# Four state heads side by side in the matmul array: a transformer block with linear attention on one core

## The chip, the cores and the metric

The kernel runs on one core of a Trainium2 chip. The core has a matmul engine (TensorE, PE in the profile; its weight loads are shown as PEld), VectorE (DVE), ScalarE (ACT), GpSimd (POOL) and a queue engine, SyncE (SP), that issues transfers. The metric is the device time of one execution in microseconds; less is better.

## The reference

A block on x of 2048 tokens by 640 features in bf16: layer norm, linear attention with 32 heads of 20 features, a residual, layer norm, a SiLU network of 1728, a residual.

```python
qkv = (x @ wqkv).reshape(B, S, 3, H, Dh)             # x: layer norm of the input
pq, pk = q @ w_phi, k @ w_phi                         # per head, 20 x 20
phi_q = concat([softmax(pq), softmax(-pq)])
phi_k = concat([softmax(pk), softmax(-pk)])
kv = einsum("bhsf,bhsd->bhfd", phi_k, v); z = phi_k.sum(s)
o = (phi_q @ kv) / (phi_q @ z + 1e-6)
h = x0 + o @ wo
out = h + silu(layernorm(h) @ w1) @ w2
```

## The kernel before

Tokens lie in 16 tiles of 128. The kernel is a list of small operations (`op_..`), and the string `ORDER` names them one after the other; each word appends its instructions to the queues of the engines that they use, so this one string fixes the order on PE, DVE, ACT, POOL and SP alike. An engine works its own queue strictly in that order. A word's last part can choose an engine or a queue: `lk.2.3.a` loads wk slice 2 from ACT's queue, `lk.2.3.s` from SP's. A transfer signals completion on one of eight counters, which are given out in turn; a transfer that gets a counter a second time first waits on its own engine's queue for the counter's last transfer to land.

Loads: `lx` (x tiles), `lk`, `lv` (slices of the k and v weights, 128 of the 640 input features each), `lp` (w_phi, 40-byte rows), `lq` (q weights, transposed by the transfer), `lo`, `l1`, `l2`, `lh`.

*First stage.* The per-head matrices w_phi are folded into the k and q weights: PE transposes five wk slices (`wt`, L293), ACT or DVE copies them out (`wc`), PE multiplies with w_phi spread to a block matrix (`fk`, `gk`, L308), and a copy makes Wfk and Wfq (`fc`, `gc`). Every key projection needs all five slices of Wfk. `wm` (L241) are matmuls on zeros that only keep PE busy at the start. For each token tile: statistics (`st` on DVE, `rs` on POOL), normalization (`xn`), transpose on PE (`xt`) or by a transfer (`xd`); key projection `kp` and value projection `vp` (both L336); exponentials of both signs on ACT (`ke`, L358); sums and reciprocals on DVE (`kr`, L366, L369); normalization on POOL (`kn`, L376). The state product `cc` (L394) adds kv over all tokens: for each sign and five column groups, two halves of the array (64 columns each) take 64 of the 640 features and multiply them with the values of four heads that these features touch, 84 columns. It also computes products between different heads; `km` (L404) masks them away and writes KVBD, with a column for the softmax sums of the queries.

*Second stage.* `qp` (L414) projects queries (128 features by 512 tokens), `qe` (L424) takes exponentials of both signs. The query-state product `dp` (L448) runs in two row halves of 64 features, 88 columns each, ten pairs a token tile, into two pairs of PSUM banks, one for each sign. `dw` on DVE combines the signs (L461, L462, L464 reads the negative pair, L468 the positive one), `dr` (L477) inverts, `do` (L483) scales, `td` transposes by a transfer, `op` (L510) multiplies with wo, `oa` (L519) adds the residual, `sq`, `sr`, `hn`, `hd` make the second norm and its transpose.

*Network.* `up` (L581, and L591 for the last 64 features), `ua` (L603), `yp` and `yh` (L627, L642), `yo` and `yz` (add and store).

PSUM has eight banks; a pool of four pairs hands them out.

Of the kernel before, what the change touches and what calls it, by code (L numbers as in the profile page):

```python
# [25 lines left out]
lx.0.1.s lk.4.5.a lp.s lk.3.4.a lx.1.2.s lk.2.3.a mk ta wt.4 wc.4.a wt.3 wm.256 st.0 rs.0.1 wt.2 ph  # L26
wm.256 wc.3.a lx.2.4.s wc.2.a fk.4 wm.256 fc.4.a st.1 lv.3.5.a xn.0.v wm.256 wm.256 wm.256 wm.256
st.2 lk.1.2.s wt.1 wc.1.v fk.2 lk.0.1.s rs.1.2 lx.4.8.s wt.0 wc.0.v xt.0 lv.0.3.s xc.0.v rs.2.3
xn.2.v xn.1.v mc st.3 rs.3.4 st.5 st.4 st.6 fc.2.a rs.4.6 fk.1 st.7 fc.1.a wm.256 fk.0 wm.256
lx.8.12.s st.8 st.9 fk.3 st.11 st.10 wm.512 fc.0.a rs.6.8 rs.8.10 xt.2 fc.3.a xt.1 xc.2.a xn.9.v  # L30
kp.0 ke.0 xc.1.a xn.3.a kp.2 lq.0 lq.4 vp.2 lx.12.16.s st.13 vc.2.a vp.0 vp.1 xt.3 xn.5.a xn.8.v
vc.0.a xn.4.a vc.1.a xc.3.a xn.7.a st.12 ke.2 kp.1 rs.10.12 kr.0 vp.3 vc.3.a mo rs.12.14 ke.1 kn.0
xd.5 kp.5 ke.5 xn.11.v kr.5 kn.5 st.14 st.15 rs.14.16 kp.3 ke.3 gk.0 kr.3 kn.3 xd.4 kp.4 ke.4 xd.7
xd.8 kp.7 ke.7 xn.10.a gc.0.a kr.2 kn.2 xn.13.a kr.4 kr.7 kp.8 kn.4 kn.7 vp.8 vc.8.a vp.5 xd.9
l2.8.13.s kr.1 vp.4 ke.8 kr.8 kn.8 lo.s kp.9 xd.11 kp.11 vc.5.a vc.4.a xn.12.a xn.6.a xn.14.a
xn.15.a vp.9 xd.13 cc.0 cc.3 vc.9.a ke.11 ke.9 cc.5 cc.2 lq.2 xd.10 vp.13 vc.13.v xd.6 vp.10 vc.10.a
kp.13 ke.13 kp.10 ke.10 lq.3 gk.3 vp.7 kp.6 cc.4 cc.8 vc.7.a cc.7 kr.11 ke.6 gc.3.v xd.14 lq.1 kr.13
kn.1 cc.1 kr.9 kn.11 xd.12 kp.14 ke.14 xd.15 kp.15 kn.9 ke.15 kr.6 kn.6 kr.10 kn.10 gk.1 gc.1.a
kp.12 vp.15 ke.12 kr.12 gk.2 vp.11 vc.15.a gk.4 gc.2.a gc.4.v kn.12 kr.15 vc.11.v vp.12 vc.12.a
qp.0.1 qe.0.1 vp.6 vc.6.a kn.15 kn.13 qp.0.0 kr.14 qp.0.2 vp.14 qe.0.2 cc.13 qe.0.0 cc.6 cc.9 cc.10  # L40
cc.15 cc.11 cc.12 vc.14.a kn.14 cc.14 close km.0 km.1 qp.2.2 qe.2.2 l1.2.s dp.0 dw.0.v dr.0 qp.3.2
qe.3.2 qp.1.2 dp.3 dw.3.v qe.1.2 do.0.1.p do.0.0.p td.0 dr.3 qp.1.0 qe.1.0 l1.1.s dp.1 dw.1.v dr.1
do.1.0.p do.1.1.p qp.1.1 qe.1.1 dp.2 dw.2.v qp.2.1 qe.2.1 dr.2 td.1 dp.4 do.2.0.p op.0 dw.4.v oa.0
op.1 oa.1 sq.1 do.2.1.p sq.0 td.2 dp.7 dw.7.v qp.2.0 qe.2.0 dp.5 dr.4 do.3.1.p do.3.0.p td.3
l2.4.8.s l1.0.s dw.5.v sr.0 do.4.1.p hn.0 hd.0 qp.3.1 dr.7 do.4.0.v dr.5 sr.1 hn.1 hd.1 dp.6 qe.3.1
qp.3.0 qe.3.0 dw.6.v lh.s op.3 do.5.0.p oa.3 dr.6 op.2 oa.2 do.5.1.p td.5 sq.3 sq.2 up.0.3 ua.0.3
do.7.1.p do.7.0.v td.4 l2.0.4.s dp.9 do.6.1.p up.0.2 ua.0.2 sr.2 dw.9.v dp.11 dw.11.v up.0.0 ua.0.0
sr.3 hn.3 hd.3 td.7 dp.8 hn.2 up.0.1 ua.0.1 dw.8.v dr.11 dr.9 dr.8 do.6.0.p do.8.1.p do.8.0.v op.5
oa.5 dp.10 yp.0.1 td.8 sq.5 sr.5 do.9.0.v dw.10.v op.4 oa.4 sq.4 do.11.1.v op.7 oa.7 hn.5 yp.1.0
sr.4 td.6 hd.2 do.11.0.v sq.7 hd.5 hn.4 hd.4 yp.0.0 dp.12 yh.0.0 dr.10 yp.1.1 dw.12.v yo.0 do.10.1.v  # L50
op.8 op.6 dr.12 do.10.0.p yo.1 oa.6 sq.6 sr.6 sr.7 up.1.2 do.9.1.v td.9 ua.1.2 td.10 hn.6 do.12.0.p
oa.8 sq.8 up.1.1 ua.1.1 sr.8 hn.8 hn.7 op.9 hd.6 hd.8 oa.9 sq.9 op.10 oa.10 sq.10 up.1.0 ua.1.0
up.1.5 ua.1.5 hd.7 up.1.3 ua.1.3 sr.9 hn.9 up.1.6 ua.1.6 dp.13 dw.13.v hd.9 up.2.3 ua.2.3 up.1.4
dp.15 dw.15.v dr.15 do.15.1.p ua.1.4 yp.4.0 dr.13 td.11 up.2.1 op.11 yp.4.1 ua.2.1 oa.11 dp.14
yh.1.0 dw.14.v do.12.1.p sr.10 do.15.0.p hn.10 yp.2.0 up.2.4 ua.2.4 td.15 td.12 op.15 oa.15 up.2.2
ua.2.2 sq.11 yo.4 yp.5.0 yp.5.1 sq.15 sr.15 hn.15 hd.15 do.13.0.v yp.2.1 yo.2 sr.11 yp.3.0 up.2.6
ua.2.6 yh.1.1 up.2.0 ua.2.0 op.12 hn.11 yo.5 do.13.1.p td.13 dr.14 up.2.5 do.14.1.v do.14.0.p ua.2.5
yp.8.0 yp.3.1 yo.3 td.14 yp.7.1 yp.7.0 oa.12 sq.12 yp.8.1 sr.12 op.13 oa.13 op.14 hn.12 yp.6.0
yp.9.1 yp.9.0 oa.14 hd.12 sq.13 sr.13 sq.14 sr.14 hn.14 hd.14 yh.2.0 yh.2.1 hn.13 hd.13 yp.6.1 yo.8
up.4.3 up.4.2 ua.4.2 up.4.1 ua.4.1 hd.10 hd.11 up.3.6 ua.4.3 up.4.0 yo.9 up.3.1 up.3.5 ua.4.0 ua.3.1  # L60
up.3.3 ua.3.3 up.3.2 up.3.0 ua.3.2 up.3.4 yp.15.0 yo.7 yo.6 yp.14.1 ua.3.6 yh.3.0 yh.4.0 ua.3.0
yp.14.0 yo.14 ua.3.5 ua.3.4 yp.12.0 yp.11.0 yp.10.1 yp.11.1 yp.10.0 yo.10 yp.12.1 yo.12 yp.15.1
yh.3.1 yo.11 yo.15 yq.13.0 yz.13.0.a yq.13.1 yz.13.1.a
# [3 lines left out]
def kernel(  # L67
# [29 lines left out]
    HQ = [(64 * q) // DH for q in range(2 * C)]  # L97
# [8 lines left out]
    mm = ctx.enter_context(tc.tile_pool(name="mm", bufs=4, space=PSUM))  # L106

    def mm2():
        return mm.tile([P, 2, 512], F32, name="mm2")

    def mmT():
        return mm.tile([P, C, P], BF16, name="mm2")
# [26 lines left out]
    maskS = persist.tile([P, C, 4, 1], BF16, name="maskS")  # L139
    KVBD = persist.tile([P, 2, C, 4, 22], BF16, name="KVBD")  # L140
# [19 lines left out]
    def wk2():  # L160
        return late["work"]
# [32 lines left out]
    def op_mc():  # L194
        nc.gpsimd.memset(maskS[:], 1.0)
        for lo in (0, 64):
            m = maskS[lo : lo + 64, :, :, 0]
            nc.gpsimd.affine_select(
                out=m, in_=m, compare_op=ALU.is_ge, fill=0.0,
                base=0, pattern=[[64 - 3 * DH, C], [-DH, 4]], channel_multiplier=1,  # L200
            )
            nc.gpsimd.affine_select(
                out=m, in_=m, compare_op=ALU.is_gt, fill=0.0,
                base=DH, pattern=[[3 * DH - 64, C], [DH, 4]], channel_multiplier=-1,
            )
        for s in range(2):
            nc.gpsimd.tensor_copy(KVBD[:, s, :, :, 21], maskS[:, :, :, 0])

# [17 lines left out]
    def op_lq(c):  # L226
        nc.sync.dma_start_transpose(wTq[:, :, c * P : (c + 1) * P], A_wqkv[c * P : (c + 1) * P, 0:D])
# [11 lines left out]
    def op_wm(n=512, ps=None):  # L239
        ps = mm2() if ps is None else ps  # L240
        nc.tensor.matmul(ps[:, 0, 0:n], ident[:], warm[:, 0:n], start=True, stop=True)  # L241
        return ps
# [82 lines left out]
    def op_gc(ce, eng="a"):  # L325
        copy(
            eng,
            Wfq[:, ce, :].rearrange("p (r a k) -> p a r k", r=C, a=2),
            tl["gk", ce][:, :, 0:320].rearrange("p a (r k) -> p a r k", r=C),
        )  # L330
# [13 lines left out]

    def op_vc(t, eng="a"):
        copy(
            eng,
            Vps[t % NV][:].rearrange("p (a h) c -> p a h c", a=2)[:, :, :, 0:DH],
            tl["vp", t][:, :, 0:320].rearrange("p a (h f) -> p a h f", f=DH),
        )  # L350
# [21 lines left out]
    def op_kn(t):  # L372
        Ek3 = tl["ek", t][:].rearrange("p s (h f) -> p (s h) f", f=DH)
        Sk = tl["sk", t]
        n = H if t == T - 1 else 2 * H
# [3 lines left out]
        if n == H:  # L379
            nc.vector.tensor_tensor(  # L380
                Ek3[:, n:], Ek3[:, n:], Sk[:, n:].unsqueeze(2).to_broadcast([P, n, DH]), op=ALU.mult,
            )

    def op_cc(t):
        Ek, Vp = tl["ek", t], Vps[t % NV]
        if "kv" not in tl:
            kv = mm2()
            tl["kv"] = [kv[:, s, 0:420].rearrange("p (r j c) -> p r j c", r=C, j=4) for s in range(2)]
        kv = tl["kv"]
        for s in range(2):  # L390
            for r in range(C):
                for a in range(2):
                    q, lo = C * a + r, 64 * a
                    nc.tensor.matmul(  # L394
                        kv[s][lo : lo + 64, r, :, :].rearrange("p j c -> p (j c)"),
                        Ek[:, s, 64 * q : 64 * q + 64],
                        Vp[:, HQ[q] : HQ[q] + 4, :].rearrange("p h c -> p (h c)"),
                        start=(t == 0 and r == 0),
                        stop=(t == T - 1),
                        skip_group_check=True,  # L400
                    )

    def op_km(s):
        nc.vector.tensor_tensor(  # L404
            KVBD[:, s, :, :, 0:21], tl["kv"][s], maskS[:].to_broadcast([P, C, 4, 21]), op=ALU.mult,
        )
# [3 lines left out]
    def op_qp(g, i):  # L410
        ps = mm2()
# [29 lines left out]
    def op_dp(t):  # L441
        g, i = t // GT, t % GT
        ps = [mm2(), mm2()]
        for s in range(2):
            for r in range(C):
                for a in range(2):
                    lo = 64 * a
                    nc.tensor.matmul(  # L448
                        ps[s][:, a, HQ[r] * 22 : (HQ[r] + 4) * 22],
                        EqT[g][lo : lo + 64, s, r, i * P : (i + 1) * P],  # L450
                        KVBD[lo : lo + 64, s, r, :, :].rearrange("p j c -> p (j c)"),
# [245 lines left out]
```

## Time and profile before

| | us |
|---|---|
| median of three runs (241.56 to 242.15) | 242.07 |
| span of the profiled execution, first to last instruction | 239.3 |
| first matmul starts | 1.52 |
| first key projection starts | 11.04 |
| last state product group starts | 66.22 |
| first query-state product starts | 70.58 |
| state products, busy, 320 matmuls | 6.7 |
| query-state products, busy, 320 matmuls | 9.1 |

In the page, a line of section 5 gives a group's busy time and mean ns of one instruction. A matmul's mean ns is its way through the array, and neighbours overlap; what a group costs is read from the timeline, as the distance from its start to the start of the next group. In a timeline line the first number is the start, the second the length, both in us; ACTq and SPq are the issuing of transfers. A wait line reads: total us, times, longest.

### The profile page before, as it was taken

The page shows a single profiled execution, that of the slowest core. Times are in us where ns is not written, and L with a number is a line of the kernel's source. Part 1 is how long each engine was busy: PE and PEld are TensorE (multiplying, and loading weights), DVE is VectorE, ACT ScalarE, POOL GpSimd, SP SyncE. Part 2 cuts the span into 40 slices and gives each one's busy share as a digit, 9 for nine tenths or more (in the row PEclk, how much of TensorE's full clock was granted, in tenths as well). Part 3 has the DMA queues.
Part 4 walks back from the last instruction along what each step waited for, and adds up shares of the span by engine and source line. Part 5 has one row for each costly group of instructions (what it writes and reads, how often), then busy time and mean ns, then how long its engine had stood idle before and what let it go on. Part 6 is the DMA issues. An engine that isn't in the chain of part 4 may idle for free.

```text
span 239.3 us, 5227 instructions
## 1 busy us (share of the span) xinstructions
PE 232.3 (97%) x2149; PEld 150.4 (63%) x2164; DVE 131.9 (55%) x253; ACT 108.6 (45%) x158; POOL 93.5 (39%) x183
## 2 busy tenths in 40 slices
PE   6989999999999999999999999999999999999995
PEld 2867777776574555877655455565577686456762
DVE  3999799887629999899653153424023410001033
ACT  4779997675566756733035531141312023270000
POOL 5868899978902456715145005022122200000000
PEclk9999999999999999999999999999999999999999
DMA  7995896700001659735244300202221390000012
GB/s 202 327 242 96 226 203 100 190 9 0 3 3 24 157 119 234 182 61 85 56 106 82 63 3 2 53 30 55 55 58 20 78 153 0 0 3 0 27 58 82
DMA packets 42808, 20.60 MB, mean 86 GB/s; under 512 B 34336, under 2 KB 42272, under 8 KB 42784
## 3 DMA queue, kind: packets, MB, share of 16 engines
q1 hardware_dynamic: 41792, 19.29, 35.9%
q10 hardware_dynamic: 992, 0.98, 1.2%
q8 instruction: 17, 0.28, 0.5%
q14 instruction: 7, 0.06, 0.1%
HBM read 9.61 MB, written 2.62 MB: 51 GB/s over the span
## 4 chain that ended last, share of the span: by engine, by line
PE 85%; DVE 7%; DMA 5%; issue 1%; ACTq 0%; ACT 0%; DVEq 0%
PE mm L581 24%; PE mm L627 24%; PE mm L336 17%; PE mm L510 8%; PE mm L414 5%; DMA wv<-in_A_wqkv_dram 3%; PE mm L394 3%; DVE u L464 2%; DVE u L468 2%; PE mm L448 2%; DMA wk<-in_A_wqkv_dram 2%; PE mm L591 1%; PE mm L642 1%; DVE w L461 1%; PE mm L308 1%
## 5 line engine op out<-in xcount | busy, mean ns | idle before, releaser
L581 PE MATMUL mm<-HnT,w 128*128 128x512 bf16 (+1 forms) x317 | 58.5, 336 | 0.4
L627 PE MATMUL mm<-w,shT 128*128 128x320 bf16 (+2 forms) x415 | 58.5, 299 | 0.2 <-issue 0.2
L603 ACT ACTIVATE shT<-mm 128x1024 bf16<-128x1024 f32 (+2 forms) x29 | 27.6, 963 | 51.8 <-PE mm L581 44.8
L627 PEld LDWEIGHTS <-shT 128*128 128x128 bf16 x416 | 39.7, 98 | 17.8 <-issue 1.3
L581 PEld LDWEIGHTS <-w 128*128 128x128 bf16 x325 | 31.3, 98 | 23.3 <-issue 0.5
L650 DVE TENSOR_TENSOR ob<-mm,X 128x640 bf16<-128x640 f32 x15 | 12.0, 817 | 50.2 <-PE mm L627 44.1
L336 PEld LDWEIGHTS <-XnT 128*128 128x128 bf16 x320 | 30.8, 98 | 12.9 <-issue 0.9
L376 POOL TENSOR_TENSOR Ek<-Ek,Sk 128x1280 bf16<-128x1280 bf16 (+1 forms) x16 | 36.8, 2325 | 3.7 <-DVE Sk L369 3.7
L483 POOL TENSOR_TENSOR o<-u,rd 128x320 bf16<-128x320 f32 x22 | 16.3, 758 | 38.8 <-DVE rd L477 30.6
L527 ACT ACTIVATE sq<-X 128x640 bf16<-128x640 bf16 x16 | 11.8, 736 | 30.0 <-DVE X L519 27.1
L424 ACT ACTIVATE EqT<-mm 128x1024 bf16<-128x1024 f32 (+1 forms) x24 | 19.7, 880 | 11.5 <-PE mm L414 11.4
L366 DVE TENSOR_REDUCE Sk<-Ek 128x64 f32<-128x1280 bf16 x16 | 23.2, 1450 | 2.8 <-ACT Ek L358 2.8
L336 PE MATMUL mm<-wv,XnT 128*128 128x320 bf16 x160 | 23.7, 299 | 0.7 <-DMA wv<-in_A_wqkv_dram 0.7
L510 PE MATMUL mm<-wo,ot 128*128 128x320 bf16 x160 | 23.5, 299 | 0.1
L414 PE MATMUL mm<-XnT,Wfq 128*128 128x512 bf16 x94 | 22.9, 379 | 0.4
L336 PE MATMUL mm<-Wfk,XnT 128*128 128x320 bf16 x160 | 23.2, 299 | 0.0
L358 ACT ACTIVATE Ek<-mm 128x640 bf16<-128x640 f32 x32 | 20.5, 730 | 4.0 <-PE mm L336 2.6
L510 PEld LDWEIGHTS <-ot 128*128 128x128 bf16 x160 | 15.5, 98 | 7.1 <-DMA ot<-o 0.3
L519 DVE SCALAR_TENSOR_TENSOR X<-mm,X 128x640 bf16<-128x640 f32 x16 | 13.0, 822 | 11.6 <-PE mm L510 11.4
L532 POOL TENSOR_SCALAR hm<-hst 128x1 f32<-128x1 f32 x16 | 3.9, 244 | 31.3 <-DVE X L519 31.3
L414 PEld LDWEIGHTS <-Wfq 128*128 128x128 bf16 x100 | 9.2, 97 | 10.2
L247 DVE BATCH_NORM_STATS2 stats<-X 128x6 f32<-128x320 bf16 x32 | 13.6, 466 | 2.7 <-DMA X<-in_A_x_dram 2.7
(74 smaller groups left out, 210.1 us busy)
## 6 DMA issues: line engine op xcount, KB each, us to landing
out_dram<-ob SPq DMA_DIRECT2D x15, 160.0 KB, 1.8
w<-in_B_w_dram SPq DMA_DIRECT2D x3, 720.0 KB, 4.6
X<-in_A_x_dram SPq DMA_DIRECT2D x3, 640.0 KB, 7.1
w<-in_B_w_dram SPq DMA_DIRECT2D x2, 640.0 KB, 5.1
w<-in_B_w_dram SPq DMA_DIRECT2D x1, 800.0 KB, 4.7
wo<-in_A_wo_dram SPq DMA_DIRECT2D x1, 800.0 KB, 7.6
wk<-in_A_wqkv_dram ACTq DMA_DIRECT2D x3, 160.0 KB, 3.5
wv<-in_A_wqkv_dram SPq DMA_DIRECT2D x1, 480.0 KB, 7.4
```

The source lines that it names most:

```text
L247: nc.vector.bn_stats(stats[:, k, :], X[:, t, k * 320 : (k + 1) * 320])
L336: nc.tensor.matmul(ps[:, half, 0:320], tok(XnT[t // GT], t)[:, c, :], W[:, c, half * 320 : (half + 1) * 320], start=(c == 0), stop=(c == C ...
L358: nc.scalar.activation(Ek[:, s, :].rearrange("p (a n) -> p a n", a=2), tl["kp", t][:, :, 0:320], AF.Exp, scale=1.0 - 2.0 * s,)
L366: nc.vector.tensor_reduce(Sk[:], tl["ek", t][:].rearrange("p s (h f) -> p (s h) f", f=DH), axis=AX.X, op=ALU.add,)
L376: nc.gpsimd.tensor_tensor(Ek3[:, 0:n], Ek3[:, 0:n], Sk[:, 0:n].unsqueeze(2).to_broadcast([P, n, DH]), op=ALU.mult,)
L414: nc.tensor.matmul(ps[:, k, :], Wfq[:, c, r * P : (r + 1) * P], XnT[g][:, c, :], start=(c == 0), stop=(c == C - 1),)
L424: nc.scalar.activation(E[:, s, rs[0] : rs[-1] + 1, :], tl["qp", g, i][:, 0 : len(rs), :], AF.Exp, scale=1.0 - 2.0 * s,)
L483: (nc.vector if eng == "v" else nc.gpsimd).tensor_tensor(tl["o", t][:, a * 320 : (a + 1) * 320].rearrange("p (h f) -> p h f", f=DH), tl["u ...
L510: nc.tensor.matmul(ps[:, half, 0:320], tl["ot", t][:, c, :], wo[:, c, half * 320 : (half + 1) * 320], start=(c == 0), stop=(c == C - 1),)
L581: nc.tensor.matmul(ps[:, i * W : (i + 1) * W], w1[:, c, fc * P : (fc + 1) * P], HnT[g][:, c, 0:W], start=(c == 0), stop=(c == C - 1), skip ...
L603: nc.scalar.activation(sh[:, a:b], tl["up", g, k][:, 0 : b - a], AF.Silu)
L627: nc.tensor.matmul(ps, shT[g][:, fc * W + i * P : fc * W + (i + 1) * P], w2[:, fc, a:b], start=first and fc == 0, stop=last and fc == FC - ...
```

## The change

- `cc`: one head is one tile of the array, 32 columns wide. The values of a head with a column of ones (21 columns) are loaded as weights and both signs of the head's exponentials pass (2 x 20 columns). Four heads, 8 apart, run in the four column tiles; eight rounds a token tile. All heads and signs gather in one bank (number 7). No product between different heads is computed here.
- `kc`, new: ACT copies that bank to SBUF as bf16, DVE transposes it in blocks of 32 x 32. `km` then spreads it with a mask over three heads, from SBUF instead of PSUM. The mask is made by other POOL operations (`mc`) and a DVE block transpose (`mt`).
- `dp`: four row tiles of 32 features instead of two of 64, two or three heads each (44 or 66 columns), into four banks at once; both signs lie in each of the four banks. 40 matmuls a token tile instead of 20.
- PSUM: no pool. The word's part after `@` names the bank; dp takes four, mostly 0 to 3.
- `gc` copies in two instructions instead of one, since the order of the query features changes (heads 8 apart share a group of 128).
- `kn` can be shared 48 to 16 or 32 to 32 of its 64 groups between POOL and DVE; four tiles use the first, one the second (before: one the second).
- `ORDER` is new for all engines. PE has 1026 more instructions; apart from cc and dp, its matmuls are the same in number and shape but for warm-up (17 instead of 16).
- In the head, the loads are issued otherwise. SP: wk slice 0, X tiles 2 and 3, wk slices 4, 1, 3, X tile 0, X tiles 12 to 15, wv 3 and 4, wv 0 to 2, X tiles 4 to 7. ACT: X tile 1, w_phi, then the table load with the first Exp (`ta`), then wk slice 2, later X tiles 8 to 11. In the built program slice 2 waits for the counter of slice 4, and SP's transfers from X tiles 12 to 15 on for the counters of X tile 1, slice 0, w_phi and X tiles 2 and 3 in turn. PE's first transposes are of slice 0, then slice 2, 4, 1, 3. The ones columns of the values (`mo`) are set first on POOL, before the masks.

The diff, cut to its core:

```diff
-lx.0.1.s lk.4.5.a lp.s lk.3.4.a lx.1.2.s lk.2.3.a mk ta wt.4 wc.4.a wt.3 wm.256 st.0 rs.0.1 wt.2 ph
-wm.256 wc.3.a lx.2.4.s wc.2.a fk.4 wm.256 fc.4.a st.1 lv.3.5.a xn.0.v wm.256 wm.256 wm.256 wm.256
...
+lx.1.2.a mo st.1 mk lk.0.1.s lp.a lx.2.4.s ta lk.2.3.a lk.4.5.s ph rs.1.2 wm.512@7 wm.512@7 wm.512@7
+wm.512@7 wm.512@7 wm.512@7 wt.0@0 wc.0.a wm.256@2 wm.256@2 wm.256@2 wm.256@2 wm.256@2 wm.256@2 wm.256@2
+wm.256@2 wm.256@2 wm.256@2 wt.2@1 wc.2.a st.2 rs.2.3 wm.256@3 wt.4@2 wc.4.a fk.0@4 fc.0.a lk.1.2.s wt.1@3
+st.3 rs.3.4 xn.1.v mc wc.1.v lk.3.4.s fk.2@6 lx.0.1.s fc.2.a wt.3@0 xt.1@1 fk.4@2 fk.1@4 fc.1.a fc.4.a
+wc.3.v fk.3@6 xn.2.v xt.2@0 xc.2.a xc.1.v xn.3.v xt.3@1 xc.3.a fc.3.v kp.1@4 kp.2@6 st.0 rs.0.1 lx.12.16.s
...
+kn.8.q cc.8 kn.6.b cc.6 cc.13 cc.10 kc lo.s qe.0.2 qp.2.1@0 km.1 km.0 qe.2.1 dp.3@2 l2.4.8.s close dw.3 dr.3
+do.3.0.p qp.1.1@6 qe.1.1 dp.1@0 dw.1 dr.1 do.1.1.p do.3.1.p l2.8.13.s qp.1.0@4 qe.1.0 td.3 dp.0@0 qp.1.2@6
+qe.1.2 qp.3.2@7 qe.3.2 qp.2.2@4 qe.2.2 do.1.0.v td.1 dw.0 dr.0 do.0.0.p do.0.1.p dp.5@0 dw.5 dr.5 do.5.1.p
+do.5.0.p qp.3.0@6 qe.3.0 dp.2@0 dw.2 op.1@4 oa.1 sq.1 dr.2 do.2.1.p td.0 sr.1 op.0@6 oa.0 dp.7@0 dw.7 sq.0
+sr.0 qp.3.1@4 hn.1.v qe.3.1 do.2.0.p td.5 op.5@6 oa.5 hn.0.v dp.6@0 dw.6 op.3@4 oa.3 l1.1.s sq.5 l1.2.s dr.6
+do.6.1.p qp.2.0@6 qe.2.0 sr.5 dp.4@0 dw.4 dr.4 hd.1 hd.0 up.0.0@4 ua.0.0 do.6.0.p do.4.0.p do.4.1.v td.2
...
     def op_cc(t):
-        for s in range(2):
-            for r in range(C):
-                for a in range(2):
-                    q, lo = C * a + r, 64 * a
-                    nc.tensor.matmul(
-                        kv[s][lo : lo + 64, r, :, :].rearrange("p j c -> p (j c)"),
-                        Ek[:, s, 64 * q : 64 * q + 64],
-                        Vp[:, HQ[q] : HQ[q] + 4, :].rearrange("p h c -> p (h c)"),
...
+        for i in range(8):
+            for k in range(4):
+                h = 8 * k + i
+                nc.tensor.matmul(
+                    mm[32 * k : 32 * k + DH + 1, KV, 0:320].rearrange("p (s q) -> p s q", s=2)[
+                        :, :, i * DH : (i + 1) * DH
+                    ],
+                    Vp[:, h, :],
+                    Ek[:, :, h * DH : (h + 1) * DH],
...
+    def op_kc():
+        nc.scalar.copy(KVT[:], mm[:, KV, 0:320])
+        nc.vector.transpose(KVF[:].rearrange("p s r d -> p (s r d)"), KVT[:])
...
     def op_dp(t):
-                for a in range(2):
-                    lo = 64 * a
-                        ps[s][:, a, HQ[r] * 22 : (HQ[r] + 4) * 22],
-                        EqT[g][lo : lo + 64, s, r, i * P : (i + 1) * P],
+                for k in range(4):
+                    lo = 32 * k
+                        ps[:, k, (8 * s + H0[r]) * 22 : (8 * s + H0[r] + NJ[r]) * 22],
+                        EqT[g][lo : lo + 32, s, r, i * P : (i + 1) * P],
+                        KVBD[lo : lo + 32, s, r, 0 : NJ[r], :].rearrange("p j c -> p (j c)"),
```

## Prediction

> **What bounds the kernel now.** I read the page's busy times first, then what TensorE (PE) waited for, then its timeline around the two products, VectorE's (DVE) timeline beside them, and the DMA views of the head.
>
> ```profile
> PE 232.3 (97%) x2149; PEld 150.4 (63%) x2164; DVE 131.9 (55%) x253; ACT 108.6 (45%) x158; POOL 93.5 (39%) x183
> PEclk9999999999999999999999999999999999999999
> ```
> ```profile
> PE mm L241 <- POOL ident masks.py:199: 1.5, 1, 1.5
> PE mm L336 <- DMA wv<-in_A_wqkv_dram: 0.7, 1, 0.7
> PE mm L293 <- DMA wk<-in_A_wqkv_dram: 0.7, 1, 0.7
> PE mm L627 <- issue: 0.2, 1, 0.2
> ```
> PE is busy 97% of 239.3 us, and all its waits are 3.1 us, nearly all in the first 15 us. So the time is PE's work, plus its head, plus about 3 us after the last matmul. Whatever shortens PE's work shortens the time, and whatever makes PE stand lengthens it.
>
> ```profile
> 6.06 0.45 PE L293 MATMUL mm<-ident,wk 128*128 128x128 bf16 x5 [0.69 <-DMA wk<-in_A_wqkv_dram]
> ...
> 11.04 2.88 PE L336 MATMUL mm<-Wfk,XnT 128*128 128x320 bf16 x20
> 13.76 0.57 PE L336 MATMUL mm<-wv,XnT 128*128 128x320 bf16 x3
> ```
> ```profile
> 66.22 3.24 PE L394 MATMUL mm<-Vp,Ek 128*64 128x84 bf16 x160
> 69.39 1.25 PE L414 MATMUL mm<-XnT,Wfq 128*128 128x512 bf16 x4
> 70.58 0.57 PE L448 MATMUL mm<-KVBD,EqT 64*128 64x88 bf16 x20
> 71.08 2.33 PE L414 MATMUL mm<-XnT,Wfq 128*128 128x512 bf16 x10
> 73.34 0.56 PE L448 MATMUL mm<-KVBD,EqT 64*128 64x88 bf16 x20
> ```
> The head ends at 11.04, when the first key projection starts; from there real work runs without a break, but for one wait for wv. The other rows price the two products (L394, L448) by the distance from a group's start to the next group's.
>
> **The PE price of the two products.** Whole-array matmuls follow each other in 0.216 us at 512 columns and 0.136 at 320 (30 in 4.08 us from 24.72): 0.417 ns a column plus 2.7. Half-array ones fall on the same line when the two halves run together: 84 columns give 37.7 ns by the line, and L394's last block is 80 pairs in 3.17 us, 39.6 each with its exit. For 88 columns the line gives 39.3, ten pairs 0.39 us; L448 takes 0.50 to the next start, so 0.11 goes into changing over.
> The state product now costs 1.65 + 1.65 + 3.17 = 6.5 us. After, 32 matmuls a token tile in eight rounds of four tiles, 40 columns each: by the line 19.4 ns a round, 16 x 8 x 19.4 = 2.5, with three exits 2.8. It saves **3.7**. The query-state product now costs 16 x 0.50 = 8.0. After, ten rounds of four a token tile, six of 44 columns (21.0) and four of 66 (30.2), 0.247, with 0.11 for the change 0.36; 16 of them 5.7. It saves **2.3**. The bounds: the line is carried below its shortest row, the 80-column passes of L308 (six matmuls, four of 140, two of 80 columns, in 0.31 us: 33 to 36 ns for the short ones). If no round is faster than that, the savings are 1.6 and 0.5, together 2.1. I take the line, 6.0, because pairs already lie on it; nothing shows more. I find 54 changes of tile shape in PE's order against 56: -0.2.
> The Trainium skill, "TensorE: Matmul & The Clock Gate", Back-to-back issue gap, speaks against part of this: starts never come closer than about 25 ns however few the columns. No row here is that short; L394's halves start 20 ns apart on the mean, so it can only hold within a tile. By it the savings would be 3.0 and 1.9, estimates, 4.9 together.
>
> **The head.** The first pass over wk needs five slices. Before, slice 2 is on ACT's queue as its third transfer, issued at 1.7, and PE uses it at 6.06; the key projection follows 5.0 us later. After, it stands on ACT's queue behind the table load (1.28 us) and the small Exp, and the built program makes it wait for the counter that slice 4 uses first. PE's order puts its transposes (wt.2) second, ahead of everything but wt.0 and warm-up, and all folded weights need them. Slice 4 is third on SP: about as L212's third there, issued at 1.72; with 0.85 MB to move ahead it lands near 6.0, so slice 2 is issued about 6.1. By then SP, which waits only for counters of early transfers, has issued 0.48 MB of slices and X0, then 0.64 of X, 0.8 of wv and 0.64 of X. What such a transfer meets is in the trace:
>
> ```profile
> 6.98 0.39 ACTq L212 DMA_DIRECT2D wv<-in_A_wqkv_dram  x1
> ```
> ```profile
> wv<-in_A_wqkv_dram ACTq DMA_DIRECT2D x1, 320.0 KB, 8.0
> ```
> ```profile
> DMA packets 785, 1.58 MB, mean 316 GB/s; under 512 B 64, under 2 KB 611, under 8 KB 785
> ## 3 DMA queue, kind: packets, MB, share of 16 engines
> q1 hardware_dynamic: 785, 1.58, 97.9%
> ```
> The last three lines are the DMA view of 6 to 11 us: a transfer issued by ACT (queue q10) at 6.98 moves nothing before 11, while SP's queue (q1), with some 1.6 MB issued before it, keeps the engines 97.9% busy. It lands at 15.0. So transfers go about in order of issue, over both queues. Slice 2 meets a like backlog. Bytes: 3.5 MB ahead and 0.16 its own; the windows moved 202 and 326 GB/s in the first two 6 us, 3.17 MB by 12, the rest at 316 takes 1.6, less up to 1 us as it shares turns with the last X. By the likeness: 6.1 + 8.0 - 1.0 for half the bytes = 13.1. I take **13.3** (12.3 to 14.5).
> From it to the first key projection: five ACT copies at 0.65, one transpose group and two DVE copies, 4.1 us with PE at its pace. PE stands for 6 us before; the first six 512-column matmuls of the trace took 2.74 us against 1.3 later, so PE starts slow, and 3.5 us of that pace make it 5.4. I take 4.8. The skill, same page, Part 1, says an idle window of 3.4 us brings half rate back; no run shows it; by it the 5.4 holds. So real work starts at 18.1 instead of 11.04: **+7.1**. wv is then there, and its wait (15.03 less 13.76 less three of 0.136) goes: -0.9. All of DVE's statistics stand behind two copies of transposed slices in DVE's queue, so they move by the same and bring no slack back.
>
> **The new waits in the second stage.** Before, the two signs lie in two PSUM pairs, and the pair of the negative ones is free after L464; the next product starts while L468 still reads the other:
>
> ```profile
> 72.97 0.85 DVE L468 TENSOR_TENSOR u<-u,mm 128x672 f32<-128x672 f32 x1
> 73.86 0.35 DVE L477 RECIPROCAL rd<-u 128x32 f32<-128x32 f32 x1
> 74.13 0.29 DVE L461 RECIPROCAL w<-mm 128x32 f32<-128x32 f32 x1
> ```
> (L468 ends at 73.82; the product of 73.34 above did not wait.) After, each of four banks holds both signs, and banks are fixed, mostly 0 to 3: the next product waits for all of L468. From the product's last start: 0.2 to its end, 2.3 of DVE (74.13 to 76.42), 0.1: 2.6. Where one query projection lies between (2.16 + 0.18) PE stands 0.25; that is three times (3 to 1, 1 to 0, 5 to 2). Three groups (qp.3.1, op.3, up.0.0) reuse a pair just evicted by DVE or ACT: 0.2 to 0.3 each. Together **1.4**; queued behind each is all PE's work. In the first stage DVE has 54 us to do (13 statistics at 1.0, 16 sums and reciprocals at 1.94, now four shares of the normalization) while PE has 53 before its last state block; eight state products are then 512 PE instructions in 1.3 us, and q8 fetches 256 at a time, 1.1 us each (0.5% of 16 x 239.3 over 17). Ends 0 and 2.5, taken 0.6: near the row, as PE never waited there.
> At no cost: the ACT copy, the DVE block transpose and two masked products between the state and dp.3 (0.45 + 0.4 + 0.7 and hand-overs, 1.9) lie beside qp.2.1's 2.16, without it they would cost 1.9; five more ACT copies (0.3 each, ACT 45% busy); memsets at POOL's start, which put ident back 0.6, covered by the wait for slice 0.
>
> **Sum.** +7.1 - 0.9 - 6.0 - 0.2 + 1.4 + 0.6 = +2.0: span 241.3. The profiled span lies 2.8 below the median 242.07; so **244.1**. The likeliest case's own range, from slice 2 (-1, +1.2), the restart (0.7), the short rounds (up to +3.9) and waits (-1.5, +1.9): 242.2 to 247.5.
>
> **Rivals.**
> 1. *Slice 2 doesn't queue* (faster). If ACT's queue gets its turn at once, its data starts 1.2 us after issue (q10's first packets are at 2.0, issue 0.8), takes about 1.1 and lands 0.8 later: 9.2, so work starts 14.0, 4.1 earlier: 240.0. It decides from 11.3 on: a landing earlier than that makes the change a gain. "DMA: Bandwidth & Descriptors", Queues, rings and completion order, in the Trainium skill has such a rule: each engine goes round the queues packet by packet. The 4 us of nothing on q10 speak against it. For it: at the start both queues moved side by side. Chance 0.29.
> 2. *The rounds keep the price of pairs, or fetches and DVE bind*: 3.9 or 2.5 more, 246.6 to 248. For it: no quarter tile is in the trace. Chance 0.12.
> 3. *The products don't run four at once at all*: then eight rounds become 32 passes, and both products lose; 32 x 19.4 ns x 16 = 9.9 us against 6.5, and 40 passes of 24.7 ns x 16 = 15.8 against 6.3: 12.9 more where 6.0 less was counted, 263. Halves do overlap, so 0.02.
>
> **Chances.** The likeliest case 0.57. Measurement can tell about 0.3%. Faster than 241.3: 0.24 from rival 1 and 0.06 from the likeliest with all terms low; within 0.3%: 0.05 and 0.09; slower: the rest, 0.56. Range 239.8 to 247.5: it leaves out the lower half of rival 1 and the end of rival 2.
>
> **What would show it.** PE's transposes of wk waiting 5 to 7 us for DMA; ACT's wk transfer landing 6 to 8 us after issue; first key projection near 18; state rounds of 19 ns, product blocks of 0.36; PE waiting on DVE's u a quarter us at a time between 75 and 110. Wrong, if slice 2 lands by 10, or the rounds stay above 30 ns.

## The result, and the profile after

The change makes the kernel slower: 248.31 us (median of 4 runs, 247.33 to 249.45) against 241.81 for the kernel before on the same chip; the ratio is 1.0287 (95% interval 1.0247 to 1.0327). The prediction said 244.1, with a range to 247.5. Its sign was right, its size was not.

A run's reported time is its span plus about 1.7 us. So the profiled execution of before (239.3) stands for 241.0, about 1 below its median, and that of after (247.7) is the slowest of the four runs, 249.45. The traces therefore differ by 8.4 us where the medians differ by 6.5. The lines below explain the 8.4; the experiments are measured against medians.

Two lines of the page after, busy times and granted clock:

```profile
PE 233.6 (94%) x2677; PEld 151.5 (61%) x2677; DVE 138.1 (56%) x255; ACT 109.1 (44%) x164; POOL 95.4 (39%) x187
...
PEclk9959999999999999999999999999999999999999
```

PE's share fell from 97% to 94% of a longer span: PE is busy 1.3 us more and stands 14.1 us instead of 7.0, so mostly waiting was added. The 5 is new: in the third slice (12.4 to 18.6 us) PE ran at about half clock. PE's waits (total us, times, longest):

```profile
PE mm L312 <- DMA wk<-in_A_wqkv_dram: 5.3, 1, 5.3
...
PE mm L482 <- DVE u L501: 1.0, 3, 0.4
PE mm L360 <- issue: 0.8, 1, 0.8
PE mm L539 <- DMA ot<-o: 0.7, 1, 0.7
PE mm L482 <- issue: 0.5, 1, 0.5
PE mm L416 <- issue: 0.3, 1, 0.3
```

The first line is the head. Its timeline, and from the DMA view of 5 to 15 us the transfer it waits for (KB, us from issue to landing):

```profile
4.89 2.34 PE L261 MATMUL mm<-warm,ident 128*128 128x256 bf16 x10
12.56 0.71 PE L312 MATMUL mm<-ident,wk 128*128 128x128 bf16 x5 [5.34 <-DMA wk<-in_A_wqkv_dram]
...
18.81 3.04 PE L360 MATMUL mm<-Wfk,XnT 128*128 128x320 bf16 x20
```
```profile
wk<-in_A_wqkv_dram ACTq DMA_DIRECT2D x1, 160.0 KB, 7.0
```

Slice 2, issued at 5.52, lands at 12.52, and the first key projection starts at 18.81, where it was at 11.04. In the trace none of the slice's packets moves before 9.05, nine tenths have moved by 10.26, and the last ends at 12.06. It still landed ahead of two transfers that SP had issued a little earlier (wv slices at 5.06, landed at 12.82; X tiles 4 to 7 at 5.49, landed at 14.36), so the order of issue holds only roughly. Then the two products:

```profile
73.52 1.30 PE L416 MATMUL mm<-Ek,Vp 128*21 128x40 bf16 x140
75.11 1.09 PE L416 MATMUL mm<-Ek,Vp 128*21 128x40 bf16 x116 [0.29 <-issue]
76.13 2.33 PE L447 MATMUL mm<-XnT,Wfq 128*128 128x512 bf16 x10
...
81.76 0.19 PE L482 MATMUL mm<-KVBD,EqT 32*128 32x44 bf16 x2
82.24 0.45 PE L482 MATMUL mm<-KVBD,EqT 32*128 32x44 bf16 x38 [0.29 <-DVE u L501]
```

The last state block takes 2.6 us from 73.52 to the query projection at 76.13; PE stands in the middle of it for nothing that another engine did ("issue"). The query-state product starts, and stops after two matmuls until VectorE has read the previous one's banks.

PE's whole time can be cut up without gaps: from the start of each weight load to the next, summed by function. From the first key projection to the last matmul:

| PE time, us | before | after | difference | predicted |
|---|---|---|---|---|
| head: start of the first key projection | 11.04 | 18.81 | +7.8 | +7.1 |
| key and value projections, with wv's wait, fetches | 44.32 | 44.72 | +0.4 | -0.9 + 0.6 |
| state product | 6.47 | 5.08 | -1.4 | -3.7 |
| query-state product, with its waits | 7.70 | 9.53 | +1.8 | -2.3 + 1.4 |
| everything else | | | -0.2 | -0.2 |
| sum | | | +8.4 | +2.0 |

Behind the last matmul both take 2.97 us.

### The profile page after: what moved, and what is told of

Read it like the earlier page. It is cut to its first block, busy times and chain, and to the rows that moved or that the text cites. A ratio compares the mean times of both kernels' runs of the same rounds, so it can differ in the third digit from the quotient of the medians.

```text
span 247.7 us, 6302 instructions
## 1 busy us (share of the span) xinstructions
PE 233.6 (94%) x2677; PEld 151.5 (61%) x2677; DVE 138.1 (56%) x255; ACT 109.1 (44%) x164; POOL 95.4 (39%) x187
## 4 chain that ended last, share of the span: by engine, by line
PE 84%; DMA 7%; DVE 5%; issue 2%; SPq 0%; DVEq 0%
PE mm L656 23%; PE mm L610 22%; PE mm L360 18%; PE mm L539 7%; PE mm L447 5%; DMA wk<-in_A_wqkv_dram 4%; PE mm L482 2%; PE mm L416 2%; PE mm L327 2%; DMA ot<-o 2%; DVE u L498 1%; DMA HnT<-hn 1%; PE mm L669 1%; DVE u L501 1%; PE mm L620 1%
## 5 line engine op out<-in xcount | busy, mean ns | idle before, releaser
L403 POOL TENSOR_TENSOR Ek<-Ek,Sk 128x1280 bf16<-128x1280 bf16 (+2 forms) x16 | 34.7, 2195 | 4.5 <-DVE Sk L396 1.8
L512 POOL TENSOR_TENSOR o<-u,rd 128x320 bf16<-128x320 f32 x26 | 20.0, 785 | 39.3 <-DVE rd L506 28.5
L360 PE MATMUL mm<-Wfk,XnT 128*128 128x320 bf16 x160 | 23.9, 299 | 0.8 <-issue 0.8
L498 DVE TENSOR_TENSOR u<-mm,w 128x672 f32<-128x672 f32 x16 | 13.7, 857 | 1.3 <-DVE w L496 0.2
```

What stands on the lines that cost most here:

```text
L360: nc.tensor.matmul(ps[:, half, 0:320], tok(XnT[t // GT], t)[:, c, :], W[:, c, half * 320 : (half + 1) * 320], start=(c == 0), stop=(c == C ...
L403: nc.gpsimd.tensor_tensor(Ek3[:, 0:n], Ek3[:, 0:n], Sk[:, 0:n].unsqueeze(2).to_broadcast([P, n, DH]), op=ALU.mult,)
L498: nc.vector.tensor_tensor(u[:], A[1][:, :, :, 0:21], w[:].unsqueeze(3).to_broadcast([P, 4, 8, 21]), op=ALU.mult,)
L512: (nc.vector if eng == "v" else nc.gpsimd).tensor_tensor(tl["o", t][:, a * 320 : (a + 1) * 320].rearrange("p (h f) -> p h f", f=DH), tl["u ...
```

## Experiments

All line numbers inside an experiment's fences are its own. Times are medians; ratios are to the kernel before, on the same chip.

### The head: where slice 2 stands

```diff
- lp.a lx.2.4.s ta lk.2.3.a
+ lk.2.3.a lp.a lx.2.4.s ta
```

> One word of the order is moved: wk slice 2 is issued on ACT's queue ahead of w_phi and of the table load, everything else is as in the changed kernel. Theory A (the loss is the late place of slice 2 in the order of issue): it is issued before 2 us instead of 5.5, lands by 5.5 instead of 12.5, the first key projection starts at 11 to 12 instead of 18.8, and the time falls by 6.5 to 7.8 us, from 248.3 to about 241. Rival B (something else in the head is as late: slices 1, 3, the statistics or the copies): the key projection moves by less than 3 us and the time stays above 245. Rival C (what stage 1 loses in the head it gets back later, so the head is free): the key projection moves, but the time falls by less than half of it.

Measured: 242.74 us, ratio 1.0055 (1.0025 to 1.0084). Slice 2 was issued at 1.22 and landed at 5.15; PE did not wait for it.

```profile
12.43 2.90 PE L362 MATMUL mm<-Wfk,XnT 128*128 128x320 bf16 x20
```

The key projection came 6.4 us earlier and the distance stayed to the end (6.45 at the last instruction). Theory A, with one amendment: 5.6 us between medians, a little less than forecast, since 12.43 is held by w_phi, now issued later (0.6), and by VectorE's normalizations (1.5). So one word is 5.6 us of the loss, and with it mended the kernel is still 1.3 us behind the kernel before, of which its head explains 0.5 (12.43 for 11.04, less wv's wait of 0.86). The two products, which were to bring 4 to 5 us net with their new waits, bring nothing.

The reverse, in the kernel before:

```diff
- lx.1.2.s lk.2.3.a mk ta wt.4 wc.4.a wt.3
+ lx.1.2.s mk ta wt.4 wc.4.a lk.2.3.a wt.3
```

> The kernel before, with one word moved: wk slice 2 is issued on ACT's queue behind the table load and the copy of slice 4 (about 5 us) instead of at 1.7; products and everything else as before. By then SP has issued X tiles, two slices and up to 1.3 MB more. Theory A (the place of slice 2 in the order of issue costs the same in any kernel, since PE is the bound behind the head): it lands at 11.5 to 13.5, the first key projection starts at 16.5 to 18.5 instead of 11.04, and the time rises by 5.0 to 7.5 us, to 246.5 to 249. Rival B (the loss comes from the head together with the changed kernel's tighter first stage, in which VectorE has 5 us more to do; the kernel before has slack to take it up): the key projection moves as much, but the time rises by less than 4 us.

Measured: 246.98 us, ratio 1.0246 (1.0202 to 1.0290).

```profile
11.89 0.71 PE L293 MATMUL mm<-ident,wk 128*128 128x128 bf16 x5 [6.57 <-DMA wk<-in_A_wqkv_dram]
...
17.76 2.47 PE L336 MATMUL mm<-Wfk,XnT 128*128 128x320 bf16 x17
```

Issued at 4.92, landed at 11.84; the key projection moved by 6.7, wv's wait of 0.86 went, and the span rose by exactly the rest, 5.9. Theory A: the price of a late slice is the same in either kernel.

Is it the order of issue, or ACT's queue? The large transfers that SP had issued around slice 2 go to ACT's queue, behind it:

```diff
- wc.0.a
+ wc.0.a lx.12.16.a lv.3.5.a lv.0.3.a lx.4.8.a
...
- lx.12.16.s
...
- lv.3.5.s lv.0.3.s
...
- lx.4.8.s
```

> Slice 2 is issued as late as in the changed kernel (on ACT's queue, behind the table load), but the four large transfers that SP issued before slice 2 could move (X tiles 12 to 15, two parts of wv, X tiles 4 to 7, 2 MB) now stand on ACT's queue behind slice 2 and the first copy. Theory A (transfers go about in order of issue, slice 2 waits for what was issued before it): with only the small early loads ahead it lands 2.5 to 4 us after its issue, at 8 to 9.5 instead of 12.5, and the key projection starts at 13.5 to 15.5; the later wv may cost some of it again, so the time is 243 to 247. Rival B (ACT's queue, or its place behind the table load, makes a transfer slow whatever is in flight): it still lands 6 to 8 us after issue, the key projection stays at 18 to 19 or later and the time at 248 or above.

Measured: 242.13 us, ratio 1.0037 (1.0006 to 1.0069).

```profile
11.60 2.91 PE L362 MATMUL mm<-Wfk,XnT 128*128 128x320 bf16 x20
```

Slice 2 now waits for another counter, that of X tile 1, and was issued at 3.79, not as late as meant; it landed at 7.20, 3.4 us later instead of 7.0, and the key projection started at 11.60. Theory A: ACT's queue moves a slice as fast as any when little was issued before it. The feared loss by the later wv did not come. With wv's wait of 0.86 counted, this head is 0.3 us ahead of the kernel before's, and yet the median is 0.7 us behind it: what the change does behind the head brings nothing. (In the profiled execution, at 243.6 us the second longest of ten, PE also waited 2.3 us for transfers of the second norm.)

### The clock, and where its gain went

```diff
- wt.2@1
+ wm.256@2 wm.256@2
...
+ wm.256@2 wm.256@2 wt.2@1
```

There are 48 new words.

> 48 more 256-column matmuls on zeros are put on PE ahead of the transposes of slice 2, about 5.3 us of work in a wait of 5.3 us; the loads are unchanged, so slice 2 lands at 12.5 as before. Theory A (PE's clock falls while it stands and the restart at half rate is what made the head 0.7 us later than predicted): the row of the granted clock shows no 5, the transposes come every 56 instead of 107 ns, the first key projection starts at 17.0 to 17.8 instead of 18.8 and the time falls by 1.0 to 1.8 us, to about 247. Rival B (ACT's copies and DVE's, not PE's pace, set the time from slice 2 to the key projection): the clock stays up, but the key projection comes at 18.5 to 18.9 and the time stays within 0.4 us.

Measured: 249.66 us, ratio 1.0349 (1.0276 to 1.0421). The clock row has no 5, the transposes take their 56 ns, and with slice 2 landing at 11.42 in this execution the key projection starts at 15.55: 4.1 us behind the landing (4.1 again in the next experiment) instead of 6.3 (5.8 to 6.2 in four other executions of the same head). So the slow restart costs 1.7 to 2.2 us, as much as theory A said or more. Yet the time did not fall. The median says little here: two of the four runs show a mean granted clock of 0.993 all the same (250.6 and 250.95 us), the other two 1.0 (247.85 and 248.73, the latter profiled), and even these lie within the range of the kernel after. The trace shows where the lead of 3.3 us went, first in a wait for the transfer that transposes a normalized tile, then in the last state block:

```profile
28.66 2.89 PE L366 MATMUL mm<-wv,XnT 128*128 128x320 bf16 x20 [1.45 <-DMA XnT<-xn]
...
70.96 1.46 PE L422 MATMUL mm<-Ek,Vp 128*21 128x40 bf16 x160
73.26 0.63 PE L422 MATMUL mm<-Ek,Vp 128*21 128x40 bf16 x60 [0.84 <-DVE Ek L413]
75.12 0.42 PE L422 MATMUL mm<-Ek,Vp 128*21 128x40 bf16 x36 [1.23 <-issue]
```

PE got to the block 2.6 us earlier (0.8 had come back where the kernel after stands for "issue" in the projections, at 51) and stood for VectorE's share of the normalization, then for "issue"; it came out at 75.70, 0.4 us ahead of the kernel after. I formed the theory that VectorE now bounds the first stage, and took its shares away:

```diff
-        if n < 2 * H:
-            nc.vector.tensor_tensor(
                Ek3[:, n:], Ek3[:, n:], Sk[:, n:].unsqueeze(2).to_broadcast([P, 2 * H - n, DH]), op=ALU.mult,
            )
```

> The kernel with 48 more warm-up matmuls, and in addition VectorE's shares of the normalization of the keys' exponentials are left out (five token tiles keep 16 or 32 of their 64 groups unnormalized). This takes some 6 us off VectorE in the first stage. With the warm-up alone the first key projection came 3.3 us earlier than in the changed kernel, yet the time did not fall (249.7 against 248.3). Theory A (VectorE, whose statistics start behind slice 2 and whose work had grown by these shares, sets the end of the first stage, and PE's slow restart is hidden behind it): now PE's gain comes through, the last state product ends at 71 to 73 instead of 75.5 and the time falls by 2 to 4 us, to 246 or below. Rival B (the lost gain is due to instruction fetch and waits for transfers only): the last state product still ends above 74.5 and the time stays within 1 us.

Measured: 249.29 us, ratio 1.0325 (1.0282 to 1.0368).

```profile
70.99 1.96 PE L418 MATMUL mm<-Ek,Vp 128*21 128x40 bf16 x220
75.05 0.42 PE L418 MATMUL mm<-Ek,Vp 128*21 128x40 bf16 x36 [2.10 <-issue]
```

The wait on VectorE is gone and "issue" has grown by as much. My theory fell; rival B held. The stall ends with an instruction fetch. Queue q8 moves 16 KB at a time, 21 times in the kernel after for PE's 5354 instructions, so some 256 instructions each: here it begins one at 72.62 and PE goes on at 75.05; in the kernel with 48 more, 72.81 and 75.12; after, 72.77 and 75.11. So PE runs on 2.3 to 2.4 us after a fetch of 256 instructions has begun (2.9 in the kernel with the early slice, 65.84 to 68.77), whatever VectorE does. In the kernel after it begins before the block, in these two inside it, as 96 more PE instructions would move every boundary of 256. The test is a warm-up of exactly 256 instructions:

```diff
- wm.256@2 wm.256@2
+ wm.96@2 wm.96@2
...
```

It replaces the 48 by 128 words.

> The warm-up of the kernel with 48 more matmuls in another cut: 128 more matmuls of 96 columns instead of 48 of 256, about as long. With their loads they are exactly 256 PE instructions, so the boundaries of the 256-instruction blocks that q8 fetches lie at the same places of the work as in the changed kernel; 48 (96 instructions) had moved them. In the changed kernel the fetch before the last state product's block began at 72.77, ahead of the burst, and PE stood 0.5 us in it; with 48 more, 1.2 us, and without VectorE's shares 2.1 us, the fetch beginning inside the burst. Theory A (a fetch takes 2.3 to 2.9 us from its first packet until PE goes on, a burst eats a block in 2.1, and where the boundary falls decides what is lost): the clock stays up as with 48, the first key projection starts at 15.5 to 16.8, the stall in the last state block is back to 0.3 to 0.9 us, and the time falls from 249.7 to 246.5 to 248.3. Rival B (where boundaries fall does not count; PE's earlier start is lost to engines or transfers): PE stands 1.2 us or more in the last state block and the time stays at 249 or above.

Measured: 247.61 us, ratio 1.0218 (1.0164 to 1.0272).

```profile
71.36 1.29 PE L428 MATMUL mm<-Ek,Vp 128*21 128x40 bf16 x140
73.19 1.09 PE L428 MATMUL mm<-Ek,Vp 128*21 128x40 bf16 x116 [0.53 <-issue]
```

The fetch begins at 70.84, before the block; the stall is 0.53 and the block is cut after the same 140 recorded matmuls as in the kernel after. (The expectation's 2.1 us for a block of 256 instructions is the time of all 512 of the eight products; at 4.17 ns each, 256 last 1.07.) The longer warm-up holds PE 1.4 us beyond the landing (11.18 to 12.60), so the key projection starts at 16.67, 1.1 later than with 48. Yet PE comes out of the state block 1.5 us earlier, at 74.21: the block takes 2.85 us instead of 4.74, and of the lead of 2.1 on the kernel after 1.9 are still there at 73. This is theory A: what a lead is worth depends on where the boundaries fall. The size is less sure. The profiled executions, both at a granted clock of 1.0, differ by 1.0 us (246.0 and 247.0); the medians differ by 2.05, but two of the four runs with 48 words had the lower clock. Against the kernel after, the median is only 0.7 lower, and the intervals of the two ratios overlap.

### The state product's pace

> The state product issues its 32 matmuls a token tile in another order: sixteen rounds of two column tiles instead of eight rounds of four; same matmuls, same result. Theory A (a tile's starts are 25 ns apart at least, and once PE's queue of instructions is used up TensorE takes one instruction in 4.17 ns, eight to a round of four, 33 ns): with four instructions a round the pace of issue needs only 16.7 ns, so all rounds of two take 25 ns, the first as the last; the state product costs 16 x 16 x 25 = 6.4 instead of 5.1 us, and the time rises by about 1.3 us to 249.6. Rival B (a short pass in a quarter tile takes 33 ns whenever it follows many others): rounds of two also go to 33 ns, 8.5 us, time about 251.7. Rival C (the columns' line of 19.4 ns holds and something else slowed the rounds of four): 5.0 us and no change.

```diff
-        for i in range(8):
-            for k in range(4):
+        for a, i, k in [(a, i, k) for a in (0, 2) for i in range(8) for k in (a, a + 1)]:
```

Measured: 247.64 us, ratio 1.0273 (1.0221 to 1.0325). None of the three numbers was met. From a block's second token tile on, one takes 268 to 316 ns as pairs and 266 to 318 as fours, where no fetch and no end of a block falls in; the first takes 260 as pairs (16.3 ns a round of two) and 190 as fours (23.7 a round of four). The sixteen cost 5.5 against 5.1 us. So there is no floor of 25 ns between the starts in a tile, and behind the first 32 matmuls it does not matter how many tiles share the work: 32 matmuls settle at 267 ns, 8.35 each.

Columns or instructions?

```diff
+                n = 1 if "kv" in tl else 2
-                        :, :, i * DH : (i + 1) * DH
+                        :, 0:n, i * DH : (i + 1) * DH
-                    Ek[:, :, h * DH : (h + 1) * DH],
+                    Ek[:, 0:n, h * DH : (h + 1) * DH],
```

> After the first token tile the state product passes only the positive sign's 20 columns instead of both signs' 40 (it leaves out the negative sign's state of 15 of the 16 tiles). Instructions and tiles stay. Theory A (once PE's queue of instructions is drained, the state product goes at the pace at which instructions come, 8.35 ns a matmul with its load, whatever the columns): a token tile of 32 matmuls stays at about 267 ns, and the first two of a block at about 190 each; the sixteen cost 4.9 to 5.2 us as before. Rival B (the columns set the pace; pairs at 16.3 ns a round lay just on 40 columns at 0.417 ns): 32 matmuls fall to 140 to 180 ns, the sixteen to about 3 us.

Measured, with half the columns (249.06 us, one run):

```profile
73.56 1.28 PE L417 MATMUL mm<-Ek,Vp 128*21 128x20 bf16 x140
75.18 1.07 PE L417 MATMUL mm<-Ek,Vp 128*21 128x20 bf16 x116 [0.34 <-issue]
```

The form says 20 columns, and nothing else has changed: 190 ns for the first, 267 inside, 5.07 us in all. Theory A. The weights' columns:

```diff
+                n = 8 if "kv" in tl else DH + 1
-                    Vp[:, h, :],
+                    Vp[:, h, 0:n],
```

> After the first token tile the state product loads 8 instead of 21 columns as weights (it leaves out 13 of the 21 rows of the state in 15 of the 16 tiles). Theory A (the pace is that of instructions, load and matmul 4.17 ns each): a token tile of 32 stays at 267 ns inside a burst, the first two at 190, the sixteen near 5.1 us. Rival B (the weights' columns set the pace: 21 columns at 0.4 ns are 8.4 ns): 32 matmuls fall below 200 ns inside a burst, the sixteen to 3.5 us or less.

Measured: 267 ns inside a block, 5.05 us in all (249.28 us, one run). Theory A again. The pace belongs to the instructions: 8.35 ns for a load with its matmul, 4.17 each if they share it evenly, which no run here separates.

### VectorE behind the query-state product

```diff
-        nc.vector.tensor_tensor(u[:], u[:], A[0][:, :, :, 0:21], op=ALU.add)
```

> VectorE's addition of the positive sign's products is left out after the changed kernel's query-state product (the attention output lacks the positive sign's part); about 0.85 us of VectorE less a token tile, and the four banks come free that much earlier. Theory A (three products wait for VectorE to have read both signs from the same four banks): the three waits of 0.29 to 0.43 us, 1.0 us together, are gone or below 0.1 in all, and nothing takes their place before 95 us. Rival B (another engine or the instruction stream is as late there): the waits stay above 0.5 us in all under another name. The times of single runs are not compared for this.

Measured (247.31 us, one run):

```profile
81.28 0.47 PE L482 MATMUL mm<-KVBD,EqT 32*128 32x44 bf16 x40
...
83.94 0.47 PE L482 MATMUL mm<-KVBD,EqT 32*128 32x44 bf16 x40
```

The waits on VectorE are gone, and thirteen of the sixteen products run through in 0.40 us; the first still stands for "issue". Theory A, and it is worth more than the 1.0 us the wait view names: the sixteen products fall from 9.53 to 7.07 us. With the key projection at the same 18.8 us, the last matmul ends 2.5 us earlier. The wait view counts only what is left after the first two matmuls have run and stopped; and the wait for ot at 112 (0.7 of the 2.5, called a DMA's) went too, so it was VectorE's lag that had made that transfer late.

### Two other orders

```diff
- lp.a lx.2.4.s ta lk.2.3.a lk.4.5.s
+ lp.a lk.2.3.s lx.2.4.s ta lk.4.5.s
...
- wm.256@2 wm.256@2 wm.256@2 wm.256@2 wm.256@2
...
- wt.2@1 wc.2.a st.2 rs.2.3
+ wt.2@1 wc.2.a xn.1.v st.2 rs.2.3
...
- st.3 rs.3.4 xn.1.v mc
+ st.3 rs.3.4 mc
...
- fk.3@6 xn.2.v xt.2@0
+ fk.3@6 fc.3.a xn.2.v xt.2@0
...
- fc.3.v
```

> A head of another order, everything behind it as in the changed kernel: wk slice 2 is the second transfer on SP's queue (w_phi keeps its early place on ACT's), five of the ten warm-up matmuls before its transposes are left out, VectorE normalizes token tile 1 before it makes the statistics of tile 2, and ACT instead of VectorE makes the last copy of Wfk. Theory A (with an early slice the head is set by w_phi's landing and by VectorE's row of work behind it, 6.2 us from 6.6 to 12.8 in the kernel with the early slice): the block matrix starts at about 5.1 instead of 6.6 and VectorE has 0.8 less to do, so the first key projection starts at 10.3 to 11.3 instead of 12.4, and the time is 1.0 to 2.0 us below that kernel's 242.7: about 241.2, the kernel before's. Rival B (beyond the slice nothing in the head counts, the first stage is set elsewhere): the key projection moves, but the time stays within 0.6 us of 242.7.

Measured: 242.61 us, ratio 1.0058 (1.0030 to 1.0086); key projection at 12.05. The block matrix did start at 5.21, but PE then waited 0.7 for VectorE's copy of a slice and 0.7 for a normalization, so the head moved by only 0.4, the time stayed that of the kernel with the early slice, and theory A was not tested.

```diff
- kp.6@4 gk.0@2 gc.0.a vp.14@0 vc.14.a ke.6 kr.8 kr.10 qp.0.0@2
- qe.0.0 qp.0.2@6 l2.0.4.s qp.0.1@0 qe.0.1 vp.10@4 kr.6 vc.10.a kn.13.p kn.10.q vp.8@2 vc.8.a
- cc.14 cc.11 cc.9 cc.7 kn.8.q cc.8 kn.6.b cc.6 cc.13 cc.10
+ kp.6@4 cc.9 gk.0@2 gc.0.a vp.14@0 cc.7 vc.14.a ke.6 kr.8 kr.10 qp.0.0@2 cc.14
+ qe.0.0 qp.0.2@6 l2.0.4.s qp.0.1@0 cc.11 qe.0.1 vp.10@4 kn.13.p cc.13 kr.6 vc.10.a kn.10.q vp.8@2 vc.8.a
+ kn.8.q cc.10 cc.8 kn.6.b cc.6
```

> On the kernel with the other head, five of the last eight state products are moved ahead singly between projections, to where their exponentials are already normalized; the last three stay as a burst of 192 instead of 512 instructions. Theory A (the burst outruns the instruction fetch and goes at the pace of issue): the stall of 0.9 us in it is gone or below 0.2; each single product costs 0.19 plus some 0.12 for leaving, 0.31, against 0.27 inside the burst, 0.2 us more for five; VectorE's last normalization ends near 68 and may hold the last product by up to 0.3; in all 0.3 to 0.9 us less than 242.6, 241.7 to 242.3. Rival B (VectorE's end sets the time of the last product anyway): the stall goes, but a wait on VectorE of the same size stands in its place and the time stays within 0.2 us of 242.6.

Measured: 242.44 us, ratio 1.0035 (1.0005 to 1.0066).

```profile
69.60 0.38 PE L417 MATMUL mm<-Ek,Vp 128*21 128x40 bf16 x32
70.45 0.66 PE L417 MATMUL mm<-Ek,Vp 128*21 128x40 bf16 x64 [0.48 <-ACT Vp L169]
```

The fetch stall is gone, as both theories said, and a wait of 0.48 has come, not on VectorE but on ACT's copy of a value tile. A gain of 0.2 us over the last kernel lies inside both intervals: inconclusive. The three longest of its twelve runs (243.97 to 244.65 us, the first of them profiled) are also the three with a mean granted clock of 0.993; the other nine, at 0.999 or 1.0, took at most 242.62. No version here beats the kernel before.

## Why the prediction was wrong

**The head was right.** It was priced at +7.1 less 0.9 for wv: 6.2. The landing was forecast for 13.3 from one likeness (a transfer on ACT's queue that moved nothing before what SP had issued) and came at 12.5; in seven other executions with the same loads it came between 11.2 and 13.0. The key projection was forecast for 18.1 and came at 18.8, since the restart took 6.3 us, not 4.8. I had the slow pace of the first matmuls in view and took less than all of it. Moving the slice alone, in either kernel, gives 5.6 to 5.9 us. The Trainium skill, "TensorE: Matmul & The Clock Gate", Part 1, says that a long idle window brings half rate back; the trace agrees (5.3 us of waiting, then transposes every 107 instead of 56 ns). What I did not see is that a lead won in the head can be lost again later: with 48 more words 1.45 us of it went into the wait for a transposed tile and most of the rest into the last state block, where a fetch stood in the way. Rival 1, the slice that doesn't queue, is refuted by the same 7.0 us.

**The state product failed.** The step was the line of 0.417 ns a column carried down to 40 columns: 19.4 ns a round, a saving of 3.7. Measured, a round of four takes 23.7 ns for the first eight rounds and settles at 33.4, by way of 40; the saving is 1.4. The columns do not set that pace: with 20 instead of 40 it stayed the same. I had bounded it by the shortest passes of the trace (33 to 36 ns, a saving of 1.6) and chosen the other end because pairs of halves lay on the line. The nearest row to a short pass was the short pass, not the pair. The floor of 25 ns that the Trainium skill, "TensorE: Matmul & The Clock Gate", Back-to-back issue gap, states gave 3.0 and came closer, but not by what happens: with pairs, a tile's starts are 16.3 ns apart. Rival 2 (rounds that keep the price of pairs) had the right outcome for this product with a chance of 0.12.

**The query-state product failed twice.** A product was taken at 0.36 instead of 0.50; undisturbed it costs 0.397, and before it cost 0.48 on the mean: 1.3 saved, not 2.3. And the waits were taken at 1.4 and are 3.2 (9.53 less 16 times 0.397), of which 2.5 went with VectorE's addition. The mechanism was as told: four banks hold both signs, so the next product waits for all of L501. But I charged three waits, and not the products that start, stop and start again, nor the transfer of ot that VectorE's lag makes late.

**Instruction fetch was named and sized too low.** I wrote 512 instructions in 1.3 us against fetches of 1.1 and took 0.6, since PE had never waited there. By the wait view the stalls after are 0.8, 0.3 and 0.5 us, in the projections, the state block and the first query-state product (the last two lie in the rows of the products); about 1 us is the moving of the bytes, and PE goes on only 2.3 to 2.9 after it has begun.

So the terms were missed by +0.7 (head), +2.3 (state product), +2.7 (query-state product) and +0.7 (projections with their fetches): 6.4 us between the profiled executions. About 2 of these are the executions themselves, one below and one above its median; between medians the miss is 4.5, and by the experiments none of it is the head (5.6 to 5.9 us for the slice's place, against 6.2).

Not settled: why the first 32 matmuls of a block go at 5.9 ns each, how the 8.35 ns divide between a load and its matmul, and what makes q8 begin a fetch when it does. VectorE's part in the first stage was shown to be no bound in the kernel without its shares; that it is none in the kernel after was not tried by itself.

## What to carry to other kernels

Splitting an array into more, smaller tiles multiplies instructions, and for passes as short as these it is the instructions that cost: price a long burst by count (here 8.35 ns a matmul behind the first 32) and by the fetches that it outruns, not by columns. A transfer's place in the order of issue, over all queues, cost more here (5.6 to 5.9 us) than any other term: ask of each load what was issued before it. When a gain upstream does not arrive, look for the wait that ends at the same time in both kernels.

## What had not been expected of the hardware

Where the boundaries of 256 instructions fall made a state block of 256 matmuls take 2.85 or 4.74 us (4.64 without VectorE's shares; warm-ups of different length, all profiled at a granted clock of 1.0); 1.0 us of the difference was left at the end of the first two executions.

In the kernel after, VectorE's share of a normalization (128 x 320, two SBUF inputs) took 0.43 us where GpSimd stood still for its first half, 0.48 across the change from one operation of GpSimd to the next, and 1.47 and 2.10 where GpSimd was at its own share. The Trainium skill, "GPSIMD Engine Reference", in its table beside the SBUF interfaces, says that GpSimd contends with VectorE instructions that have two SBUF inputs; the trace agrees, with a factor of three to five.

PE's clock fell after less than the 5.3 us of waiting: in the spread kernel's profiled execution PE was busy 1.86 of the 4 us from 8 to 12, its longest stand 1.45, and the granted clock from 12 to 15 was 0.50, so that a key projection pair took 4.4 us instead of 2.7. The same kernel without the spreading, busy 2.63 of the same 4 us, kept its clock.
